# Second channel product of an MLP mixer by quarters: seven products in place of eight

## The chip, the cores and the metric

The kernel runs on one core of a Trainium2 chip. The metric is the device time of one execution in microseconds, as the median of several runs. The profile is one further execution of the same program, recorded by the hardware profiler. The engines are TensorE (PE; its weight loads are shown apart as PEld), VectorE (DVE), ScalarE (ACT), GpSimd (POOL) and SyncE (SP, which here issues transfers).

## What is computed

A linear-attention block feeds an MLP mixer. All arrays are float32; the batch is 4, with 8 heads of 48, so 384 model columns, and 768 tokens.

```
for t in range(S):                                   # per batch and head, state is 48 x 48
    cur = outer(u * k[t], v[t])
    y[t] = r[t] @ (state + cur)
    state = w[t][:, None] * state + outer(k[t], v[t])
x  = y, heads side by side                           # (4, 768, 384)
h  = relu(x^T @ w_tok1) @ w_tok2                     # w_tok1 768 x 256, w_tok2 256 x 768
u  = x + h^T
out = u + relu(u @ w_ch1) @ w_ch2                    # w_ch1 384 x 1536, w_ch2 1536 x 384
```

The change concerns the last product, relu(u @ w_ch1) @ w_ch2. Below, z is relu(u @ w_ch1).

## The kernel before

**Attention.** Tokens are cut into twelve units of 256 tokens, three to a batch. For each unit, `levels` builds a matrix of attention weights (`at`) in six doublings. A doubling is a group of small TensorE matmuls into `gram` (L246), two VectorE products that decay `k` and `r` in place (`join`, L271 and L272), and a VectorE copy under a mask out of `gram` (`pick`, L255), or a ScalarE copy for the last two. The next doubling's matmuls read the `k` and `r` that the join has written, and the join overwrites what the previous gram matmuls read. `post` then transposes k (kT, L306), forms state updates (kv_ps, L316, and twelve small VectorE operations, L333), and makes the output (y_ps, L353 and L366).

**Mixer.** `mixing(bt)` makes the pieces for one batch: `hidden` and `back` are the token products (L386, L393), `turn` transposes u into `xT`, `up` makes z, and `down` makes the output. Tokens come in three segments of 256 (SEG). For a segment, `up` runs 12 times (one 128-wide block of the 1536 hidden columns each; three matmuls of 128 x 128 weights against 256 columns, L408, and one ScalarE activation, L410, into `z`). `down` runs twice, once for each 128 tokens: 12 matmuls accumulate in one bank of PSUM, with a 128 x 128 block of z as the stationary operand and 384 columns of `wch2` moving (L417); VectorE then adds u (L421) into `o`, and SP's queue stores it (L422). z has two buffers, `o` three.

**PSUM.** Everything of the mixer, and kT of the later batches, takes turns in two banks (pool `ps_m`, tag "m"). A product can begin only when the one before the last has been read out of its bank.

**Order.** The mixer's pieces of batch bt are woven with the attention of batch bt + 1 (`woven`), in proportion to a cost written beside each piece. The framework's scheduler then fixes one order for each engine, and each engine runs its queue strictly in that order. The last batch's mixer has no attention beside it. In the first batch the four weight matrices are converted from float64 on VectorE and ScalarE (`conversion`), in scratch tiles (`d64`, `mantissa`, `exponent`), before they can be used; the first segment's down pieces are small so as to stand between conversions.

The two loops that set the order of the channel products are:

```
# first batch
pieces = downs[0][-4:] + ups[2] + downs[1] + downs[2]
# later batches
for s in range(1, S // SEG):
    pieces += ups[s] + downs[s - 1]
pieces += downs[-1]
```

Of the kernel before, what the change touches and what calls it, by code (L numbers as in the profile page):

```python
# [10 lines left out]
f32 = mybir.dt.float32  # L11
bf16 = mybir.dt.bfloat16
u8 = mybir.dt.uint8
u16 = mybir.dt.uint16
u32 = mybir.dt.uint32
# [3 lines left out]
B, H, S, D = 4, 8, 768, 48  # L19
DM = H * D  # L20
# [11 lines left out]
NJ = DCH // 128  # L32
PIECE = 512
SEG = 256


def woven(*lists):

    keyed = []
    for n, pieces in enumerate(lists):  # L40
        total, at = sum(c for c, _ in pieces), 0.0
        for i, (c, f) in enumerate(pieces):
            keyed.append(((at + c / 2) / total, n, i, c, f))
            at += c
    return [(c, f) for *_, c, f in sorted(keyed, key=lambda e: e[:3])]


def emit(pieces):
    for _, f in pieces:
        f()  # L50
# [3 lines left out]
def rwkv6_then_mixer(  # L54
# [23 lines left out]
    pe, dve, act, pool, sp = nc.tensor, nc.vector, nc.scalar, nc.gpsimd, nc.sync  # L78
# [41 lines left out]
    for l in range(4):  # L120
        b = 1 << l
        m = const.tile([128, 64 // b, 2 if l == 0 else b], f32, name=f"mask{l}")
# [5 lines left out]
        n, x = (T, 1) if l == 0 else (32, UC * A)  # L128
# [17 lines left out]
    bits64 = [wide.tile([128, 2 * PIECE], u32, name=f"d64_{i}") for i in range(2)]  # L146
    bits64 += [spare[:, ts(i, 2 * PIECE)] for i in range(2)]
    mantissas = [wide.tile([128, PIECE], u32, name=f"mantissa{i}") for i in range(2)]
    exponents = [wide.tile([128, 2, PIECE], u16, name=f"exponent{i}") for i in range(2)]
    rebias = const.tile([128, 1], f32, name="rebias")  # L150
    dve.memset(rebias, -896.0 * 128)

# [38 lines left out]
    xs = {}  # L191
# [183 lines left out]
                (0.01, lambda: load_rkw(i + 3)), (0.01, lambda: load_v(i + 3))]  # L375


    def mixing(bt):
        h1 = mpool.tile([128, DTOK // 128, DM], f32, name="h1", bufs=1)
        xT = mpool.tile([128, DM // 128, S], f32, name="xT", bufs=1)  # L380
        zs, sums = {}, {}

        def hidden(i, c):
            if c == 0:
                sums[i] = ps_m.tile([128, DM], f32, name="h1_ps", tag="m")
            pe.matmul(sums[i], wtok1[:, c, ts(i, 128)], xs[bt][:, c, :], start=(c == 0), stop=(c == C - 1))  # L386
            if c == C - 1:
                act.activation(h1[:, i, :], sums.pop(i), AF.Relu)

        def back(c):  # L390
            ps = ps_m.tile([128, DM], f32, name="h_ps", tag="m")
            for i in range(DTOK // 128):
                pe.matmul(ps, wtok2[:, i, ts(c, 128)], h1[:, i, :], start=(i == 0), stop=(i == DTOK // 128 - 1))  # L393
            x = xs[bt]
            dve.tensor_add(x[:, c, :], x[:, c, :], ps)  # L395

        def turn(c):
            ps = ps_m.tile([128, DM // 128, 128], f32, name="xT_ps", tag="m")
            for m in range(DM // 128):
                pe.transpose(ps[:, m, :], xs[bt][:, c, ts(m, 128)], ident)  # L400
            act.copy(xT[:, :, ts(c, 128)], ps)  # L401

        def up(s, jt):
            if jt == 0:
                zs[s] = mpool.tile([128, NJ, SEG], f32, name="z")
            ps = ps_m.tile([128, SEG], f32, name="z_ps", tag="m")
            for m in range(DM // 128):
                pe.matmul(ps, wch1[:, m, ts(jt, 128)], xT[:, m, ts(s, SEG)],  # L408
                          start=(m == 0), stop=(m == DM // 128 - 1))
            act.activation(zs[s][:, jt, :], ps, AF.Relu)  # L410

        def down(s, n, jts=range(NJ)):
            if jts[0] == 0:
                sums[s, n] = ps_m.tile([128, DM], f32, name="h2_ps", tag="m")
            ps = sums[s, n]
            for jt in jts:
                pe.matmul(ps, zs[s][:, jt, ts(n, 128)], wch2[:, jt, :], start=(jt == 0), stop=(jt == NJ - 1))  # L417
            if jts[-1] == NJ - 1:
                c = s * (SEG // 128) + n
                o = mpool.tile([128, DM], f32, name="o", bufs=3)  # L420
                dve.tensor_add(o, xs[bt][:, c, :], ps)  # L421
                sp.dma_start(out[bt, ts(c, 128), :], o)  # L422
# [7 lines left out]
        downs = [[(7.7, lambda s=s, n=n: down(s, n)) for n in range(SEG // 128)] for s in range(S // SEG)]  # L430
        if bt == 0:
            downs[0] = [(1.3, lambda n=n, jt=jt: down(0, n, range(jt, jt + 2)))
                        for jt in range(0, NJ, 2) for n in range(SEG // 128)]
# [12 lines left out]
    p0, p1, p2 = post(0), post(1), post(2)  # L446
# [7 lines left out]
    for bt in range(B):  # L454
        if bt == 0:
            emit(woven(turned, to_ch[:2]))
            both = [f for e in zip(ups[0], ups[1]) for f in e]
            emit(woven(both, to_ch[2:7]))
            emit(woven(downs[0][:-4], to_ch[7:]))
            pieces = downs[0][-4:] + ups[2] + downs[1] + downs[2]  # L460
        else:
            hiddens, pieces, ups, downs = mixing(bt)
            pieces = [(3.9, lambda h=h: emit(h)) for h in hiddens] + pieces + ups[0]
# [41 lines left out]
```

## Time and profile before

| | |
|---|---|
| median of 3 runs | 659.64 us (659.58 to 660.15) |
| the profiled execution's own time | 661.45 us |
| its span, first to last instruction | 659.7 us |
| mean granted TensorE clock | 0.974 |
| PE busy | 622.7 us, 94% |
| DVE busy | 273.5 us, 41% |
| ACT busy | 194.9 us, 30% |

The busy time of an engine is the union of its instructions' records. A matmul's record runs from its start to its modelled end and overlaps the next one's, so the spacing of matmuls says more than their length. In a row of the costliest groups stand the line, the engine, the operation, out<-in, the shapes and the count; then busy us and mean ns of one; then the engine's idle time just ahead of them and what ended it. In a row of the timeline stand the start, the busy time, and the merged instructions with their count. A row of the waits has who waited for whom, the sum in us, how often, and the longest.

### The profile page before, as it was taken

Reading aid. Unit: us, or ns where it says so; the run is one execution under the profiler, and the core shown is the slowest. Engines: PE = TensorE matmul, PEld = TensorE weight load, DVE = VectorE, ACT = ScalarE, POOL = GpSimd, SP = SyncE. Lnnn points to the kernel's source line nnn. Section 1 sums busy time; section 2 is a strip of 40 time slices with the busy share of each in tenths; the row PEclk is TensorE's granted clock in tenths of the full one; section 3 lists DMA queues with packets and bytes.
Section 4 is the critical chain, followed back from the end, with each engine's and each line's share of the span. In section 5 each row is a group of like instructions: output and inputs, shape, how many; then the busy total and the mean of one; then the engine's idle time right before and its main releaser. Section 6 shows DMA issues by size and latency. Waiting matters only on the chain.

```text
span 659.7 us, 18806 instructions
## 1 busy us (share of the span) xinstructions
PE 622.7 (94%) x8584; PEld 456.6 (69%) x8584; DVE 273.5 (41%) x618; ACT 194.9 (30%) x465; POOL 7.2 (1%) x32
## 2 busy tenths in 40 slices
PE   3889789999999899999999999999999999999997
PEld 3777557867866666787686666788687565886854
DVE  6889789935555326242252226243143111000000
ACT  7153554512350431423231313432121201230200
POOL 3000000000000000000000000000000000000000
PEclk9996779999999899999999999999999999999999
DMA  8236755501030320101202220000000000000000
GB/s 348 79 99 193 203 141 171 191 0 51 27 107 18 109 62 2 50 2 50 73 2 61 63 74 1 2 2 2 14 14 14 13 26 0 1 1 12 13 24 24
DMA packets 19375, 38.56 MB, mean 58 GB/s; under 512 B 2112, under 2 KB 12864, under 8 KB 19296
## 3 DMA queue, kind: packets, MB, share of 16 engines
q1 hardware_dynamic: 19152, 37.36, 18.0%
q8 instruction: 67, 1.10, 0.7%
q14 instruction: 12, 0.10, 0.0%
q10 hardware_dynamic: 144, 0.00, 0.0%
HBM read 32.64 MB, written 4.72 MB: 57 GB/s over the span
## 4 chain that ended last, share of the span: by engine, by line
PE 88%; DVE 5%; ACT 3%; DMA 2%; issue 1%; SPq 0%; DVEq 0%; ACTq 0%
PE z_ps L408 29%; PE h_ps L417 29%; PE gram L246 10%; PE h_ps L386 6%; PE h_ps L393 5%; PE y_ps L353 2%; PE y_ps L366 2%; PE gram L232 2%; PE kv_ps L316 2%; PE kT_ps L306 1%; ACT at L263 1%; DMA d<-in_w_ch_dram 1%; DVE r L272 1%; PE xT_ps L400 1%; DMA w<-in_rkw_dram 1%
## 5 line engine op out<-in xcount | busy, mean ns | idle before, releaser
L408 PE MATMUL z_ps<-xT,wch 128*128 128x256 f32 x864 | 197.2, 384 | 0.6 <-ACT xT L401 0.6
L417 PE MATMUL h_ps<-wch,z 128*128 128x384 f32 x576 | 192.9, 491 | 0.8 <-ACT kT L307 0.8
L408 PEld LDWEIGHTS z_ps<-xT,wch 128*128 128x128 f32 x864 | 160.8, 190 | 23.7 <-ACT xT L401 0.8
L417 PEld LDWEIGHTS h_ps<-wch,z 128*128 128x128 f32 x576 | 107.8, 190 | 72.0 <-ACT kT L307 1.2
L410 ACT ACTIVATE z<-z_ps 128x256 f32<-128x256 f32 x144 | 55.1, 383 | 172.2 <-PE z_ps L408 172.2
L421 DVE TENSOR_TENSOR o<-x,h_ps 128x384 f32<-128x384 f32 x24 | 13.3, 554 | 200.6 <-PE h_ps L417 200.6
L246 PEld LDWEIGHTS gram<-r,k 48*64 48x64 f32 x3840 | 74.7, 155 | 23.3 <-issue 16.1
L246 PE MATMUL gram<-r,k 48*64 48x32 f32 x3840 | 81.8, 237 | 7.7 <-issue 3.1
L271 DVE TENSOR_TENSOR k<-k,decay 112x512 f32<-112x512 f32 x36 | 24.9, 691 | 58.8 <-PE gram L246 58.8
L386 PE MATMUL h_ps<-x,wtok 128*128 128x384 f32 x96 | 40.4, 571 | 1.7 <-ACT x L372 1.6
L263 ACT COPY at<-gram 16x256 f32<-16x256 f32 (+1 forms) x72 | 31.3, 434 | 32.9 <-PE gram L246 31.5
L393 PE MATMUL h_ps<-h,wtok 128*128 128x384 f32 x96 | 36.5, 508 | 3.4 <-DVE x L395 1.7
L271 DVE TENSOR_TENSOR k<-k,w 112x512 f32<-112x512 f32 x36 | 24.7, 687 | 35.5 <-PE gram L246 30.2
L333 DVE SCALAR_TENSOR_TENSOR state<-state,w_chunk,kv_ps 128x48 f32<-128x48 f32 x160 | 29.1, 258 | 11.0 <-PE kv_ps L316 10.9
L255 DVE COPY_PREDICATED at<-mask,gram 128x512 f32<-128x512 uint8 x36 | 32.3, 897 | 0.0
L238 DVE COPY_PREDICATED at<-mask,gram 128x512 f32<-128x512 uint8 x24 | 16.3, 723 | 37.2 <-PE gram L232 37.1
L232 PE MATMUL gram<-rp,kp 48*64 48x64 f32 x768 | 21.3, 250 | 10.5 <-ACT kp L220 8.0
L232 PEld LDWEIGHTS gram<-rp,kp 48*64 48x64 f32 x768 | 17.5, 155 | 17.8 <-ACT kp L220 10.4
L386 PEld LDWEIGHTS h_ps<-x,wtok 128*128 128x128 f32 x96 | 19.9, 219 | 13.9 <-issue 3.3
L272 DVE TENSOR_TENSOR r<-r,w 112x512 f32<-112x512 f32 x36 | 24.5, 685 | 6.7 <-ACT rp L216 6.7
L393 PEld LDWEIGHTS h_ps<-h,wtok 128*128 128x128 f32 x96 | 16.6, 189 | 14.8 <-DVE x L395 2.9
L359 ACT COPY seen<-y_ps 128x2 f32<-128x2 f32 x12 | 1.9, 160 | 79.4 <-PE y_ps L353 79.4
(55 smaller groups left out, 388.0 us busy)
## 6 DMA issues: line engine op xcount, KB each, us to landing
d<-in_w_ch_dram SPq DMA_DIRECT2D x10, 512.0 KB, 4.6
vt<-in_v_dram SPq DMA_DIRECT2D x12, 384.0 KB, 3.7
out_dram<-o SPq DMA_DIRECT2D x24, 192.0 KB, 1.9
x<-in_w_ch_dram SPq DMA_DIRECT2D x8, 512.0 KB, 4.2
w<-in_rkw_dram SPq DMA_DIRECT2D x18, 192.0 KB, 3.4
k<-in_rkw_dram SPq DMA_DIRECT2D x18, 192.0 KB, 3.2
r<-in_rkw_dram SPq DMA_DIRECT2D x18, 192.0 KB, 3.4
d<-in_w_tok_dram SPq DMA_DIRECT2D x4, 512.0 KB, 9.5
```

Of the source, the lines that this page charges most:

```text
L232: pe.matmul(g[cols, q, ts(a, T)], L["kp"][rows, tokens], L["rp"][rows, tokens], start=True, stop=True)
L246: fours(lambda q, j, rows, cols: pe.matmul(g[cols, q, ts(ca, 32)], k_[rows, ds(ca * 128 + j * T, T)], right[rows, ts(2 * ca + j, 32 // b), ...
L255: dve.copy_predicated(out=dst, data=g.rearrange("p q (m b) -> p q m b", b=b), mask=masks[l].rearrange("p x t -> p (x t)").rearrange("p (m ...
L263: act.copy(at[p:p + b, :, :, n * 2 * b + b:(n + 1) * 2 * b], g[p:p + b, :, :, ts(n, b)])
L271: dve.tensor_mul(left, left, wv[:, :, 1].unsqueeze(2).to_broadcast([ROWS, n, b]))
L272: dve.tensor_mul(right, right, wv[:, :, 0].unsqueeze(2).to_broadcast([ROWS, n, b]))
L333: dve.scalar_tensor_tensor(new[:, a], state[bt, g][:, a], L["w"][:, c, a, j:j + 1], got[:, a], op0=ALU.mult, op1=ALU.add)
L386: pe.matmul(sums[i], wtok1[:, c, ts(i, 128)], xs[bt][:, c, :], start=(c == 0), stop=(c == C - 1))
L393: pe.matmul(ps, wtok2[:, i, ts(c, 128)], h1[:, i, :], start=(i == 0), stop=(i == DTOK // 128 - 1))
L408: pe.matmul(ps, wch1[:, m, ts(jt, 128)], xT[:, m, ts(s, SEG)], start=(m == 0), stop=(m == DM // 128 - 1))
L410: act.activation(zs[s][:, jt, :], ps, AF.Relu)
L417: pe.matmul(ps, zs[s][:, jt, ts(n, 128)], wch2[:, jt, :], start=(jt == 0), stop=(jt == NJ - 1))
```

## The change

The segment's product z (256 x 1536) by `wch2` (1536 x 384) is cut into quarters: z into a11, a12, a21, a22 (128 tokens by 768 hidden columns each), `wch2` into w11, w12, w21, w22 (768 by 192). The Strassen-Winograd scheme forms the four output quarters from seven products of quarters in place of eight. Each of the seven is six matmuls of a 128 x 128 block against 192 columns.

- `begin` makes three sums of z's quarters (s1, s2, s4) and one in place (a21 becomes a11 - a21): four VectorE operations of 768 elements a partition.
- `weight_sums` makes three sums of the weight's quarters once (t1, t2, t4), of 1152 elements a partition, in the scratch that the conversion has left; `weight_difference` turns w12 into w22 - w12 in place.
- p1, p4, p2, p5, p6, p7, p3 are the products, in that order, with a VectorE add or two behind each; p1 is copied out of PSUM by ScalarE first.
- The very first segment (batch 0, segment 0) keeps the undivided product. The other eleven are cut.
- z has one buffer for the first segment and one for all others; the first one's space then holds the sums. `o` is one buffer for a whole segment.
- The downs of a segment now stand right behind its ups.
- The bits, mantissas and exponents of the conversion lie in one tile, `scratch`.

```
+    def weight_sums():
+        t1, t2, t4 = w_sums
+        dve.tensor_sub(t1, w12, w11)
+        dve.tensor_sub(t2, w22, t1)
+        dve.tensor_sub(t4, w21, t2)
+
+    def weight_difference():
+        dve.tensor_sub(w12, w22, w12)
...
-                zs[s] = mpool.tile([128, NJ, SEG], f32, name="z")
+                zs[s] = halves[int((bt, s) != (0, 0))].rearrange("p (j t) -> p j t", j=NJ)
...
+        def quarters(s):
+            z = halves[1].rearrange("p (j t) -> p j t", j=NJ)
+            a11, a12, a21, a22 = (z[:, ts(j, HJ), ts(i, 128)] for i in range(2) for j in range(2))
...
+            def begin():
+                dve.tensor_add(s1, a21, a22)
+                dve.tensor_sub(s2, s1, a11)
+                dve.tensor_sub(s4, a12, s2)
+                dve.tensor_sub(a21, a11, a21)
+
+            def product(a, b):
+                ps = ps_m.tile([128, HM], f32, name="q_ps", tag="m")
+                for j in range(HJ):
+                    pe.matmul(ps, a[:, j, :], b[:, j, :], start=(j == 0), stop=(j == HJ - 1))
+                return ps
...
+            def p1():
+                o = L["o"] = mpool.tile([128, 2, DM], f32, name="o", bufs=1)
+                x = L["x"] = xs[bt][:, ts(s, 2), :]
+                act.copy(m1, product(a11, w11))
+                dve.tensor_add(o[:, 0, :HM], x[:, 0, :HM], m1)
...
+            def p4():
...
+                dve.tensor_add(o[:, 1, :HM], x[:, 1, :HM], product(a22, t4))
...
+            def p2():
...
+                dve.tensor_add(o[:, 0, :HM], o[:, 0, :HM], product(a12, w21))
...
+            def p5():
...
+                dve.tensor_add(o[:, :, HM:], x[:, :, HM:], product(s1, t1).unsqueeze(1).to_broadcast([128, 2, HM]))
...
+            def p6():
...
+                dve.tensor_add(u2, m1, product(s2, t2))
+                dve.tensor_add(o[:, 0, HM:], o[:, 0, HM:], u2)
...
+            def p7():
...
+                dve.tensor_add(u3, u2, product(a21, w12))
+                dve.tensor_add(both, both, u3.unsqueeze(1).to_broadcast([128, 2, HM]))
+                store(1)
...
+            def p3():
...
+                dve.tensor_add(o[:, 0, HM:], o[:, 0, HM:], product(s4, w22))
+                store(0)
+
+            return [(0.01, begin)] + [(1.96, p) for p in (p1, p4, p2, p5, p6, p7, p3)]
...
-            pieces = downs[0][-4:] + ups[2] + downs[1] + downs[2]
+            weight_sums()
+            pieces = downs[0][-4:] + [(0.01, weight_difference)] + downs[1] + ups[2] + downs[2]
...
-            for s in range(1, S // SEG):
-                pieces += ups[s] + downs[s - 1]
-            pieces += downs[-1]
+            for s in range(S // SEG):
+                pieces += ups[s] + downs[s]
```

**How the order moves.** The rows below are the built programs' own order; a count is of matmuls in the code. z_150 is the buffer of z that the cut segments use, z_149 the one that then holds sums, and `scratch` holds t1, t2 and t4; so `q_ps<-scratch,z_150` is p4, `q_ps<-scratch,z_149` p5 or p6, `q_ps<-wch_144,z_149` p3, and `q_ps<-wch_144,z_150` p1, p2 or p7.

TensorE at the first segment of the second batch, with the attention of the third (r_86, k_89), before:

```order
L246 MATMUL gram<-r_86,k_89 64x32 x32
L408 MATMUL z_ps<-xT,wch_143 128x256 x9
L316 MATMUL kv_ps<-vt,kT 64x48 x32
L408 MATMUL z_ps<-xT,wch_143 128x256 x9
L246 MATMUL gram<-r_86,k_89 64x32 x32
L408 MATMUL z_ps<-xT,wch_143 128x256 x9
```

And changed:

```order
L247 MATMUL gram<-r_86,k_89 64x32 x32
L427 MATMUL z_ps<-xT,wch_143 128x256 x6
L461 MATMUL q_ps<-wch_144,z_150 128x192 x6
L317 MATMUL kv_ps<-vt,kT 64x48 x32
L461 MATMUL q_ps<-scratch,z_150 128x192 x6
L247 MATMUL gram<-r_86,k_89 64x32 x32
L461 MATMUL q_ps<-wch_144,z_150 128x192 x6
L461 MATMUL q_ps<-scratch,z_149 128x192 x6
L247 MATMUL gram<-r_86,k_89 64x32 x32
```

The products stand where the next segment's ups stood, so z is multiplied as soon as it is complete, and a product of six matmuls lies on each side of the attention's groups.

VectorE at the same place, before, from the second join of that unit on:

```order
L271 TENSOR_TENSOR k_89<-k_89,decay 112x256x2
L272 TENSOR_TENSOR r_86<-r_86,decay 112x256x2
L255 COPY_PREDICATED at_95<-mask_1_116,gram 128x256x2
L273 TENSOR_TENSOR decay<-w_92 112x128
L330 COPY state<-kv_ps 128x192
L333 SCALAR_TENSOR_TENSOR state<-state,w_chunk,kv_ps 128x48 x12
L271 TENSOR_TENSOR k_89<-k_89,w_92 112x128x4
```

And changed, from `decay` on (the three rows ahead of it are the same):

```order
L274 TENSOR_TENSOR decay<-w_92 112x128
L453 TENSOR_TENSOR z_149<-z_150 128x768
L454 TENSOR_TENSOR z_149<-z_149,z_150 128x768
L456 TENSOR_TENSOR z_150<-z_150 128x6x128
L455 TENSOR_TENSOR z_149<-z_150,z_149 128x768
L471 TENSOR_TENSOR o<-x,z_149 128x192
L331 COPY state<-kv_ps 128x192
L334 SCALAR_TENSOR_TENSOR state<-state,w_chunk,kv_ps 128x48 x6
L475 TENSOR_TENSOR o<-x,q_ps 128x192
L334 SCALAR_TENSOR_TENSOR state<-state,w_chunk,kv_ps 128x48 x4
L272 TENSOR_TENSOR k_89<-k_89,w_92 112x128x4
```

The four sums of z, and the adds of p1 and p4, have come between one join and the next.

VectorE in the first batch, behind the last conversion, before:

```order
L271 TENSOR_TENSOR k_88<-k_88,decay 112x256x2
L272 TENSOR_TENSOR r_85<-r_85,decay 112x256x2
L255 COPY_PREDICATED at_94<-mask_1_116,gram 128x256x2
L273 TENSOR_TENSOR decay<-w_91 112x128
L273 TENSOR_TENSOR w_92<-decay 112x256
L272 TENSOR_TENSOR r_87<-r_87,w_93 112x512
L421 TENSOR_TENSOR o<-x,h_ps 128x384 x2
```

And changed:

```order
L272 TENSOR_TENSOR k_88<-k_88,decay 112x256x2
L390 TENSOR_TENSOR scratch<-wch_144 128x1152
L273 TENSOR_TENSOR r_85<-r_85,decay 112x256x2
L391 TENSOR_TENSOR scratch<-wch_144,scratch 128x1152
L256 COPY_PREDICATED at_94<-mask_1_116,gram 128x256x2
L392 TENSOR_TENSOR scratch<-wch_144,scratch 128x1152
...
L453 TENSOR_TENSOR z_149<-z_150 128x768
L456 TENSOR_TENSOR z_150<-z_150 128x6x128
L395 TENSOR_TENSOR wch_144<-wch_144 128x6x192
L454 TENSOR_TENSOR z_149<-z_149,z_150 128x768
L455 TENSOR_TENSOR z_149<-z_150,z_149 128x768
L441 TENSOR_TENSOR o<-x,h_ps 128x384 x2
```

The weight's sums and the first z sums stand ahead of the adds that end the first segment's undivided product.

TensorE at the end of that batch's weaving, with the third unit of the second batch (r_87, k_90), before:

```order
L353 MATMUL y_ps<-state,r_86 64x48 x32
L417 MATMUL h_ps<-wch_144,z 128x384 x6
L246 MATMUL gram<-r_87,k_90 64x32 x32
L366 MATMUL y_ps<-vt,at_95 64x48 x32
L246 MATMUL gram<-r_87,k_90 64x32 x32
L232 MATMUL gram<-rp,kp 64x64 x11
L306 MATMUL kT_ps<-ident,k_90 128x128 x8
```

And changed:

```order
L354 MATMUL y_ps<-state,r_86 64x48 x32
L247 MATMUL gram<-r_87,k_90 64x32 x32
L461 MATMUL q_ps<-wch_144,z_150 128x192 x6
L367 MATMUL y_ps<-vt,at_95 64x48 x32
L461 MATMUL q_ps<-scratch,z_149 128x192 x6
L247 MATMUL gram<-r_87,k_90 64x32 x32
L233 MATMUL gram<-rp,kp 64x64 x11
L307 MATMUL kT_ps<-ident,k_90 128x128 x8
```

Two products (p2 and p5) have come between the last two groups of gram.

More of the change, by code (lines that the diff above doesn't have):

```diff
@@ L34 @@
 SEG = 256
+HJ, HM = NJ // 2, DM // 2
 def woven(*lists):
@@ L145, in rwkv6_then_mixer @@
     spare = xpool.tile([128, C, DM], f32, name="x").rearrange("p c e -> p (c e)").bitcast(u32)
[L146 to L149, printed above, removed]
+    scratch = wide.tile([128, 8 * PIECE], u32, name="scratch")
+    bits64 = [t[:, ts(i, 2 * PIECE)] for t in (scratch, spare) for i in range(2)]
+    mantissas = [scratch[:, ts(i, PIECE)] for i in (4, 5)]
+    exponents = [scratch[:, ts(i, PIECE)].bitcast(u16).rearrange("p (two n) -> p two n", two=2) for i in (6, 7)]
     rebias = const.tile([128, 1], f32, name="rebias")
@@ L375, in post @@
                 (0.01, lambda: load_rkw(i + 3)), (0.01, lambda: load_v(i + 3))]
+    halves = [mpool.tile([128, NJ * SEG], f32, name=f"z{i}", bufs=1) for i in range(2)]
+    z_sums = [halves[0][:, ts(i, HJ * 128)].rearrange("p (j t) -> p j t", j=HJ) for i in range(3)]
+    w_sums = [scratch[:, ts(i, HJ * HM)].bitcast(f32).rearrange("p (j e) -> p j e", j=HJ) for i in range(3)]
+    parts = halves[0][:, ds(3 * HJ * 128, 3 * HM)].rearrange("p (n e) -> p n e", n=3)
+    w11, w12, w21, w22 = (wch2[:, ts(i, HJ), ts(j, HM)] for i in range(2) for j in range(2))
+    def weight_sums():
[5 more added lines that the diff above has]
+        dve.tensor_sub(w12, w22, w12)
     def mixing(bt):
@@ L410, in up, with down @@
             act.activation(zs[s][:, jt, :], ps, AF.Relu)
-        def down(s, n, jts=range(NJ)):
+        def down(n, jts):
             if jts[0] == 0:
-                sums[s, n] = ps_m.tile([128, DM], f32, name="h2_ps", tag="m")
-            ps = sums[s, n]
+                sums[n] = ps_m.tile([128, DM], f32, name="h2_ps", tag="m")
+            ps = sums[n]
             for jt in jts:
-                pe.matmul(ps, zs[s][:, jt, ts(n, 128)], wch2[:, jt, :], start=(jt == 0), stop=(jt == NJ - 1))
+                pe.matmul(ps, zs[0][:, jt, ts(n, 128)], wch2[:, jt, :], start=(jt == 0), stop=(jt == NJ - 1))
@@ L418, in down @@
             if jts[-1] == NJ - 1:
[L419 to L422, printed above, removed]
+                o = mpool.tile([128, 2, DM], f32, name="o", bufs=1) if n == 0 else sums["o"]
+                sums["o"] = o
+                dve.tensor_add(o[:, n], xs[bt][:, n, :], ps)
+                sp.dma_start(out[bt, ts(n, 128), :], o[:, n])
@@ L429, in mixing @@
         ups = [[(1.3, lambda s=s, jt=jt: up(s, jt)) for jt in range(NJ)] for s in range(S // SEG)]
[L430 to L433, printed above, removed]
+        first = [(1.3, lambda n=n, jt=jt: down(n, range(jt, jt + 2))) for jt in range(0, NJ, 2) for n in range(2)]
+        downs = [first if (bt, s) == (0, 0) else quarters(s) for s in range(S // SEG)]
         return hiddens, turned, ups, downs
@@ L459, in rwkv6_then_mixer @@
             emit(woven(downs[0][:-4], to_ch[7:]))
[L460 removed]
+            weight_sums()
+            pieces = downs[0][-4:] + [(0.01, weight_difference)] + downs[1] + ups[2] + downs[2]
         else:
             hiddens, pieces, ups, downs = mixing(bt)
[L463 to L466 removed]
+            pieces = [(3.9, lambda h=h: emit(h)) for h in hiddens] + pieces
+            for s in range(S // SEG):
+                pieces += ups[s] + downs[s]
         n = (bt + 1) * UB
```

13 lines of the change are left out of this document (added).

## The prediction

> **What bounds the kernel now.** I read the page first: busy times, the chain that ended last, the costliest groups.
>
> ```profile
> span 659.7 us, 18806 instructions
> PE 622.7 (94%) x8584; PEld 456.6 (69%) x8584; DVE 273.5 (41%) x618; ACT 194.9 (30%) x465; POOL 7.2 (1%) x32
> PE 88%; DVE 5%; ACT 3%; DMA 2%; issue 1%; SPq 0%; DVEq 0%; ACTq 0%
> L417 PE MATMUL h_ps<-wch,z 128*128 128x384 f32 x576 | 192.9, 491 | 0.8 <-ACT kT L307 0.8
> L417 PEld LDWEIGHTS h_ps<-wch,z 128*128 128x128 f32 x576 | 107.8, 190 | 72.0 <-ACT kT L307 1.2
> L421 DVE TENSOR_TENSOR o<-x,h_ps 128x384 f32<-128x384 f32 x24 | 13.3, 554 | 200.6 <-PE h_ps L417 200.6
> ```
>
> The chain is TensorE for 88%. The second channel product (L417) is 576 recorded passes; the code issues 24 outputs x 12 = 288 matmuls, so each f32 matmul runs as two passes. Busy time of pipelined passes overlaps, so I take their spacing from a stretch with nothing else in it, the last 50 us of the timeline.
>
> ```profile
> 609.50 15.70 PE L408 MATMUL z_ps<-xT,wch 128*128 128x256 f32 x72
> ...
> 625.04 31.12 PE L417 MATMUL h_ps<-wch,z 128*128 128x384 f32 x96
> ...
> 632.98 0.56 DVE L421 TENSOR_TENSOR o<-x,h_ps 128x384 f32<-128x384 f32 x1 [22.73 <-PE h_ps L417]
> 640.72 0.55 DVE L421 TENSOR_TENSOR o<-x,h_ps 128x384 f32<-128x384 f32 x1 [7.18 <-PE h_ps L417]
> ```
>
> Two outputs end 7.74 us apart; one is 24 passes, so a 384-column pass takes 322.5 ns. The 72 passes of 256 columns begin within 15.70 us less one record of 0.38 us: 15.32/71 = 215.8 ns. That is 106.7 ns for 128 columns, or 0.833 ns a column, and 2.5 ns fixed. The time of a pass goes by its columns.
>
> Then the stages, to see whether TensorE is the limit in each, and its own waits after 137 us.
>
> ```profile
> 137.00:152.00 15.00, 15.00 (x48) 8.88 (x48) 1.65 (x5) 0.38 (x1) 0.00 (x0) 1.00 0.00 0
> 152.00:242.00 90.00, 86.64 (x1803) 62.34 (x1802) 43.71 (x106) 28.14 (x68) 0.34 (x3) 0.98 0.23 68
> 242.00:402.00 160.00, 158.15 (x2264) 113.59 (x2264) 57.78 (x130) 49.23 (x122) 0.22 (x2) 1.00 0.14 39
> 402.00:562.00 160.00, 156.08 (x2053) 111.35 (x2051) 47.85 (x115) 37.28 (x89) 0.00 (x0) 1.00 0.03 9
> 562.00:657.00 95.00, 93.84 (x366) 68.60 (x363) 3.82 (x7) 14.78 (x38) 0.00 (x0) 1.00 0.03 11
> ```
>
> ```profile
> PE gram L246 <- DVE r L272: 2.3, 4, 0.6
> ...
> PE z_ps L408 <- ACT xT L401: 0.6, 2, 0.3
> ```
>
> The columns after the length are PE, PEld, DVE, ACT and POOL busy. PE is busy for 96 to 100% of every stage from 137 us on, and its seven rows of waits there (first and last shown, 2.3+2.0+1.5+1.4+0.8+0.8+0.6) hold 9.4 us. VectorE is free for two thirds of 152 to 562 us (149.3 busy of 410). So columns taken from TensorE should be time taken from the end, if VectorE's added work finds its place.
>
> **TensorE's share.** A segment of 256 tokens costs 48 passes of 384 columns now, 48 x 322.5 ns = 15.48 us. Changed, it is seven products of six matmuls, 84 passes of 192 columns. By the two numbers above one is 192 x 0.833 + 2.5 = 162.5 ns; 84 make 13.65 us. Eleven of the twelve segments change (the first stays whole): 11 x 1.83 = **20.1 us** off the path.
>
> That extrapolates 64 columns below the narrowest pass of this kind, so the weight load must fit in 162.5 ns; its record is 190 ns. The nearest rows are a start from an empty TensorE:
>
> ```profile
> L386 PEld LDWEIGHTS h_ps<-x,wtok x96: 186/190/338, 55.1 to 549.4; 128*128 128x128 f32 x96
> L386 PE MATMUL h_ps<-x,wtok x96: 486/486/1009, 55.1 to 549.7; 128*128 128x384 f32 x96
> ...
> 542.15 0.30 PEld L386 LDWEIGHTS h_ps<-x,wtok 128*128 128x128 f32 x2
> ...
> 542.16 0.91 PE L386 MATMUL h_ps<-x,wtok 128*128 128x384 f32 x2
> ```
>
> Two loads of 190 ns fit in 0.30 us: the second begins 0.11 us after the first. And the second pass begins 0.91 - 0.486 = 0.42 us after the first was issued, one pass (0.32) plus 0.10: the first pass had waited 0.10 us for its weights, not 0.19. I take a load as 0.10 to 0.11 us of occupancy and the rest as latency that overlaps. Bounds for the pass: 160 ns (columns alone) to 192 ns (a load must finish by its record before the next pass); the empty start and 215.8 ns being exactly on the line of columns put it at 162.5.
>
> A rule of the Trainium skill speaks against this: "TensorE: Matmul & The Clock Gate", Part 3, "The mechanism", has weight loads overlapping matmuls in flight only where the row group differs. By that rule each full-array pass would carry its load in front. The 215.8 ns rows, with a 128x128 load between every two passes, disagree.
>
> **VectorE's share.** Prices:
>
> ```profile
> L273 DVE TENSOR_TENSOR decay<-w 112x512 f32<-112x512 f32 x12 | 8.3, 689 | 0.3
> L273 DVE TENSOR_TENSOR w<-decay 112x256 f32<-112x256 f32 x12 | 5.0, 420 | 0.3
> L410 ACT ACTIVATE z<-z_ps 128x256 f32<-128x256 f32 x144 | 55.1, 383 | 172.2 <-PE z_ps L408 172.2
> L333 DVE SCALAR_TENSOR_TENSOR state<-state,w_chunk,kv_ps 128x48 f32<-128x48 f32 x160 | 29.1, 258 | 11.0 <-PE kv_ps L316 10.9
> out_dram<-o SPq DMA_DIRECT2D x24, 192.0 KB, 1.9
> ```
>
> 1.05 ns an element: a sum of quarters of z (768) is 0.96 us, of weights (1152) 1.36 us, a 192-wide add out of the product's bank 0.554 - 0.20 = 0.35 us. A segment adds 4 sums (3.8 us) and ten adds of which two are 384 wide (3.55+0.35 us at most), and drops two adds (1.1): +6.3 to 6.7 us. With 5.4 us for the weights VectorE rises from 273 to about 350 us. ScalarE gets one copy of 192 columns a segment, about 0.33 us by L410's row; it is far from full. The output transfers stay 24 of 192 KB; SP's queue keeps its order. There is one `o` buffer in place of three, but the next first add comes some 15 us after the store, against 1.9 us to landing. Only at the first changed segment is it close:
>
> ```profile
> 152.62 1.13 PE L246 MATMUL gram<-r,k 48*64 48x32 f32 x64
> 152.73 0.55 DVE L421 TENSOR_TENSOR o<-x,h_ps 128x384 f32<-128x384 f32 x1 [0.73 <-PE h_ps L417]
> 153.69 1.99 PE L408 MATMUL z_ps<-xT,wch 128*128 128x256 f32 x8
> ```
>
> `o` is complete at 153.3 us and would land at 155.2; product p1 takes the place of the passes at 153.69 and ends at 155.6, so no wait.
>
> The weight sums are issued behind the last conversions, into 137 to 152 us, where VectorE was busy for 1.65 of 15 us; that stretch also takes the first segment's z sums and the in-place difference (together 9.3 + 1.65 of 15). If z sums had to wait for all of the first segment's reads instead of the blocks they overwrite, some 4 us would stand on the path there: 0 to 4, and I take 0, since the order shows a second, later wait on TensorE only at the third z sum.
>
> In the other woven segments the four sums form a lump of 3.8 us in VectorE's queue, and behind it stand the add that frees p4's bank (two banks rotate, so p5 waits for it) and the attention's next join. I follow it through the first segment of the second batch, from these rows of before:
>
> ```profile
> 283.59 1.13 PE L246 MATMUL gram<-r,k 48*64 48x32 f32 x64
> 284.66 4.15 PE L408 MATMUL z_ps<-xT,wch 128*128 128x256 f32 x18
> 284.80 0.69 DVE L271 TENSOR_TENSOR k<-k,decay 112x512 f32<-112x512 f32 x1 [3.27 <-PE gram L246]
> 286.01 1.30 DVE L255 COPY_PREDICATED at<-mask,gram 128x512 f32<-128x512 uint8 x1
> 287.10 0.32 DVE L273 TENSOR_TENSOR decay<-w 112x128 f32<-112x128 f32 x1
> 288.74 1.15 PE L316 MATMUL kv_ps<-vt,kT 64*64 64x48 f32 x64
> ```
>
> TensorE: in the new order 12 up passes follow this gram, to 287.25; p1 to 289.2, kv (1.08) to 290.3, p4 to 292.2, gram to 293.3, p2 to 295.3, when p5 needs p4's bank. VectorE: free at 287.4; z is complete at about 287.9 (0.38 for the last activation by L410's row, 0.25 allowed ahead of it); four sums to 291.7, p1's add 292.1, state copy and six updates (0.18 us each by 29.1/160) to 293.5, p4's add 293.9. That is 1.4 us early. The next join ends at 295.8, its gram is wanted at 297.2. So here nothing waits. Over the eight woven segments I allow 1.5 us; the ends are 0 and 20 us (2.5 us in each, below).
>
> Something is also given back: at the end of the first batch two grams stood with only y_ps between them.
>
> ```profile
> 221.35 1.13 PE L246 MATMUL gram<-r,k 48*64 48x32 f32 x63 [0.56 <-DVE r L272]
> 223.43 0.19 PE L246 MATMUL gram<-r,k 48*64 48x32 f32 x1 [0.95 <-issue]
> ...
> 224.41 1.76 PE L306 MATMUL kT_ps<-ident,k 128*128 128x128 f32 x8 [0.27 <-DVE k L271]
> ...
> 220.00:240.00 20.00, 18.22 (x362) 12.22 (x355) 6.54 (x19) 7.00 (x17) 0.11 (x1) 0.91 0.33 100
> ```
>
> Waits of 1.8 us and a granted clock of 0.91 over 20 us (1.8 us more). Products now stand between these grams. 0 to 3.6; I take 1.5, since the 0.95 of issue is no wait for VectorE.
>
> In the last batch nothing is woven in: sums end 4.4 us after the last hidden block, p5 begins after 5.85. The very last add is 0.2 us shorter.
>
> **Sum**, against the profiled execution's 661.45 us (span 659.7): -20.1 - 0.2 + 1.5 - 1.5 = 641.1. The median of the runs, 659.64, stands 1.8 lower, so 639.3.
>
> **Rivals.** *VectorE's lump makes TensorE wait.* For it: p4's add and every join stand behind 3.8 us of sums, and the slack worked out is 1.4 us. Where twelve state updates (2.2 us) fall in as well, p5 would wait 1 to 2.5 us. 1.5 us in eight segments is 12: about 650. At 2.5 us each the whole gain is gone. Against: VectorE would still be half idle (149 + 51 of 390 us).
>
> *The weight load is the limit (slower).* If a pass cannot begin before the load's 190 ns record ends, passes come 192 ns apart: 84 x 192 = 16.1 us, +0.65 us a segment, 667 us. It decides from 15.48/84 = 184 ns on. For it: the record itself. Against: the empty start.
>
> *Loads do not overlap passes (slower).* 0.104 us in front of each: 84 x 266.5 = 22.4 against 48 x 426.5 = 20.5 us, +1.9 a segment, 681 us. The rows above exclude it nearly. It is what the rule of the Trainium skill cited above, in "TensorE: Matmul & The Clock Gate", Part 3, would make of this kernel.
>
> *The change does not do what it says*: the fixed part of a pass is larger at 192 columns, say 184 ns in all; no change, 660.
>
> **Chances.** The sum with its small terms (634 to 645): 0.75. VectorE's lump costing 6 us or more (645 to 658): 0.14. Load limit 0.05, no overlap 0.01, no change 0.03, below 634 (more given back) 0.02. The range 634 to 650 takes 0.75 and two thirds of the second case. A difference under 0.2% is about what cannot be told from none here. Faster: 0.75 + 0.02 + 0.13 = 0.90; same 0.03; slower 0.07.
>
> **What would show it.** 924 passes of q_ps, 162.5 ns apart in the tail, a quarter segment 13.65 us long there; VectorE near 350 us; few waits of q_ps on `o`. A spacing of 184 ns or more, or rows of several us "q_ps <- DVE o" or "gram <- DVE", would prove me wrong.

## The result, and the profile after

The changed kernel takes 637.45 us (median of 4 runs, 637.35 to 639.3), the kernel before 659.89 us beside it (4 runs, 659.58 to 663.98): a ratio of 0.9653, 95% interval 0.9611 to 0.9694, or 22.4 us less. The profiled execution took 637.35 us.

The page after, the lines that answer to those shown of before:

```profile
span 635.6 us, 19813 instructions
PE 605.2 (95%) x8980; PEld 508.2 (80%) x8980; DVE 341.8 (54%) x743; ACT 198.3 (31%) x476; POOL 7.2 (1%) x32
PE 90%; ACT 3%; DVE 3%; DMA 2%; issue 1%; SPq 0%; ACTq 0%; DVEq 0%
L461 PE MATMUL q_ps<-wch,z 128*128 128x192 f32 x528 | 94.9, 330 | 0.0
L461 PE MATMUL q_ps<-scratch,z 128*128 128x192 f32 x396 | 71.2, 330 | 0.2 <-ACT kT L308 0.2
L453 DVE TENSOR_TENSOR z<-z 128x768 f32<-128x768 f32 x11 | 10.5, 959 | 66.6 <-ACT z L429 66.6
```

TensorE is still the chain, now for 90%. The second channel product is 528 + 396 = 924 passes of 192 columns beside the first segment's 48 whole ones. VectorE has risen from 273.5 to 341.8 us and is no bound.

A segment of the last batch, from TensorE's timeline:

```profile
589.25 2.11 PE L461 MATMUL q_ps<-wch,z 128*128 128x192 f32 x12
591.20 2.11 PE L461 MATMUL q_ps<-scratch,z 128*128 128x192 f32 x12
593.15 2.11 PE L461 MATMUL q_ps<-wch,z 128*128 128x192 f32 x12
595.10 4.06 PE L461 MATMUL q_ps<-scratch,z 128*128 128x192 f32 x24
599.00 4.06 PE L461 MATMUL q_ps<-wch,z 128*128 128x192 f32 x24
602.90 1.46 PE L427 MATMUL z_ps<-xT,wch 128*128 128x256 f32 x6
```

The starts are what counts: 589.25 to 602.90 is 13.65 us for 84 passes, 162.5 ns each, and a product of 12 passes is 1.95 us. The two whole outputs of a segment took 15.48 us before.

TensorE's waits from 137 us to the end (who waited for whom, sum in us, times, longest):

```profile
PE h_ps L412 <- DVE x L414: 1.3, 4, 0.4
PE gram L247 <- DVE r L273: 1.2, 2, 0.6
PE z_ps L427 <- ACT xT L420: 0.5, 2, 0.3
PE kT_ps L307 <- DVE k L272: 0.4, 1, 0.4
PE xT_ps L419 <- DVE x L414: 0.3, 1, 0.3
PE q_ps L461 <- ACT kT L308: 0.2, 1, 0.2
```

They hold 3.9 us, against 9.4 before. No product waits for a bank that an add frees ("q_ps <- DVE o" isn't there), and 1.5 us of "gram <- issue" have gone.

**How kernels are compared below.** Whole times of one program differ by some us between executions. In after's two profiles the whole times are 0.9 us apart, and from the first z_ps matmul on only 0.03; e7 and e9 are 3.5 us apart, and not at all from there on. That matmul begins anywhere from 104 to 109 us, behind the conversion. So beside the medians the table gives, from each profiled execution, the time from the start of the first z_ps matmul to the end of the last matmul (end less start, "from z on"). Before's is 656.16 - 105.59; it was profiled once, and its runs scatter by about 8 us in each of the later sets.

| kernel | median us (runs) | ratio to before on the same chip, 95% | from z on, us |
|---|---|---|---|
| before | 659.89 (4) | | 550.57 |
| after | 637.45 (4) | 0.9653, 0.9611 to 0.9694 | 526.83 |
| after, again | 638.24 (6) | 0.9613, 0.9580 to 0.9645 | 526.86 |
| e1, undivided, changed order | 664.22 (12) | 1.001, 0.9982 to 1.0037 | 553.19 |
| e2, the same in small pieces | 656.90 (6) | 0.9916, 0.9885 to 0.9947 | 546.01 |
| e8, before in small pieces | 656.04 (6) | 0.9874, 0.9837 to 0.9911 | 544.91 |
| e3, eight quarter products | 657.71 (10) | 0.992, 0.9896 to 0.9943 | 546.41 |
| e4, seven products, no sums | 639.50 (6) | 0.9645, 0.9614 to 0.9676 | 527.03 |
| e5, sums doubled | 640.35 (4) | 0.9639, 0.9599 to 0.9679 | 529.97 |
| e10, doubled, p4's add behind all | 658.41 (6) | 0.9926, 0.9890 to 0.9963 | 547.36 |
| e6, passes of 96 columns | 692.85 (2) | 1.0426, 1.0360 to 1.0492 | 581.83 |
| e7, all twelve segments cut | 638.14 (6) | 0.9602, 0.9565 to 0.9638 | 526.20 |
| e9, the same, p2 ahead of p4 | 637.47 (6) | 0.9604, 0.9575 to 0.9634 | 526.20 |

E1 to e4 shared one set of runs of before (663.23 us, 21 runs), e5 to e8 another (664.55, 11), the second run of after, e9 and e10 a third (663.56, 13).

### The profile page after: what moved, and what is told of

It is laid out like the page before. It is cut to its first block, busy times and chain, and to the rows that moved or that the text cites. A ratio compares the mean times of both kernels' runs of the same rounds, so it can differ in the third digit from the quotient of the medians.

```text
span 635.6 us, 19813 instructions
## 1 busy us (share of the span) xinstructions
PE 605.2 (95%) x8980; PEld 508.2 (80%) x8980; DVE 341.8 (54%) x743; ACT 198.3 (31%) x476; POOL 7.2 (1%) x32
## 4 chain that ended last, share of the span: by engine, by line
PE 90%; ACT 3%; DVE 3%; DMA 2%; issue 1%; SPq 0%; ACTq 0%; DVEq 0%
PE z_ps L427 31%; PE q_ps L461 24%; PE gram L247 10%; PE h_ps L405 6%; PE h_ps L412 5%; PE h_ps L437 2%; PE kv_ps L317 2%; PE gram L233 2%; PE y_ps L367 2%; PE y_ps L354 2%; PE kT_ps L307 1%; ACT at L264 1%; DMA scratch<-in_w_ch_dram 1%; PE xT_ps L419 1%; DMA w<-in_rkw_dram 1%
## 5 line engine op out<-in xcount | busy, mean ns | idle before, releaser
L461 PE MATMUL q_ps<-wch,z 128*128 128x192 f32 x528 | 94.9, 330 | 0.0
L461 PEld LDWEIGHTS q_ps<-wch,z 128*128 128x128 f32 x528 | 86.1, 190 | 1.4
L461 PE MATMUL q_ps<-scratch,z 128*128 128x192 f32 x396 | 71.2, 330 | 0.2 <-ACT kT L308 0.2
L461 PEld LDWEIGHTS q_ps<-scratch,z 128*128 128x128 f32 x396 | 64.2, 190 | 1.3 <-ACT kT L308 0.6
L453 DVE TENSOR_TENSOR z<-z 128x768 f32<-128x768 f32 x11 | 10.5, 959 | 66.6 <-ACT z L429 66.6
L405 PE MATMUL h_ps<-x,wtok 128*128 128x384 f32 x96 | 39.1, 557 | 1.7 <-ACT x L373 1.6
L334 DVE SCALAR_TENSOR_TENSOR state<-state,w_chunk,kv_ps 128x48 f32<-128x48 f32 x160 | 30.5, 256 | 4.4 <-PE kv_ps L317 4.3
```

Source lines behind the costliest of these rows:

```text
L334: dve.scalar_tensor_tensor(new[:, a], state[bt, g][:, a], L["w"][:, c, a, j:j + 1], got[:, a], op0=ALU.mult, op1=ALU.add)
L461: pe.matmul(ps, a[:, j, :], b[:, j, :], start=(j == 0), stop=(j == HJ - 1))
```

## Experiments

The theory: 20.1 us are columns that TensorE no longer passes; the sums are free as long as the adds that free the banks don't stand behind them; the rest comes from what stands between the attention's groups. The rivals: the order of the pieces, the size of the pieces, or the sums costing something that another gain covers.

**Where do the 3 to 4 us beyond the columns come from: e1, e2, e8.** The diff also moves a segment's downs ahead of the next segment's ups, and replaces two pieces of 7.7 us by seven of 1.96. e1 takes the new order with the undivided product in two pieces, e2 the same in eight pieces of three matmuls; neither makes sums.

```
-        def quarters(s):
+        def undivided(s):
...
+            def whole(n, jts):
...
+                for j in jts:
+                    pe.matmul(L[n], z[:, j, ts(n, 128)], wch2[:, j, :], start=(j == 0), stop=(j == NJ - 1))
```

with jts = range(12) at a cost of 7.74 (e1) or range(j, j + 3) at 1.94 (e2).

> The changed kernel's order (downs of a segment right behind its ups, one buffer of z), but the undivided product: 24 matmuls of 384 columns in two pieces of 7.7, no sums. If the gain is the columns (theory), a segment costs 15.48 us again and the time is that of before less what the order alone gives back: 657 to 660. If a good part of the 22 us came from the order and the smaller pieces (rival), it is 640 to 652.

> As e1, but the undivided product is woven in eight pieces of three matmuls (1.9 us each, as long as one of the seven products). The trace of the change shows 2.0 us more gained in the first batch and 1.3 in the second than eleven times 1.83. If products between the attention's groups give that (theory), e2 is 1 to 3 us under e1, 655.5 to 658.5. If it came from something else, a clock dip of one execution or the order of the segments, e2 equals e1.

e8 is the kernel before, its own order kept, with the pieces cut alone:

```
-        downs = [[(7.7, lambda s=s, n=n: down(s, n)) for n in range(SEG // 128)] for s in range(S // SEG)]
+        downs = [[(1.93, lambda s=s, n=n, j=j: down(s, n, range(j, j + 3))) for n in range(SEG // 128)
+                  for j in range(0, NJ, 3)] for s in range(S // SEG)]
```

> The kernel before, in its own order, with each undivided output woven in four pieces of three matmuls in place of one of twelve. e2 had these pieces in the changed order and was 4.6 us shorter by trace than before, e1 in large pieces was not. If the size of the pieces alone does it (theory), this kernel is 4 to 6 us under before. If it takes the new order of the segments as well (rival), within 1.5 us of before.

From z on, e1 is 2.6 us above before, e2 4.6 below, e8 5.7 below; by the medians e2 is 6.3 and e8 8.5 us below, and e1 isn't told from before. E1 thus missed its 657 to 660, and e2 gained 7.3 us on e1 by the medians where 1 to 3 had been expected; e8 came as forecast by trace. So the order isn't the source; the size of the pieces is, and it is worth that without any quarter product. Where it comes from shows in 180 to 232 us, the end of the first batch. The rows of the windows are, in this order, of before, e1, e2, e8 and after; the columns behind the length are PE, PEld, DVE, ACT and POOL busy, the granted clock, the DMA share and GB/s.

```profile
180.00:232.00 52.00, 48.68 (x1057) 33.63 (x1058) 26.19 (x67) 16.75 (x40) 0.22 (x2) 0.97 0.26 74
```
```profile
180.00:232.00 52.00, 50.22 (x1076) 37.81 (x1076) 28.08 (x75) 20.43 (x51) 0.34 (x3) 0.93 0.24 67
```
```profile
180.00:232.00 52.00, 51.95 (x1065) 38.64 (x1064) 26.22 (x67) 20.62 (x51) 0.17 (x2) 1.00 0.26 71
```
```profile
180.00:232.00 52.00, 52.00 (x1044) 34.38 (x1042) 27.32 (x68) 16.75 (x40) 0.22 (x2) 1.00 0.27 74
```
```profile
180.00:232.00 52.00, 51.34 (x1190) 44.16 (x1189) 30.39 (x75) 21.01 (x54) 0.22 (x2) 1.00 0.25 71
```

Before loses 3.3 us of TensorE there and a clock of 0.97 over 52 us (1.6 us more); e1 gives up 1.8 us and 0.07 x 52 = 3.6. The three kernels with pieces of 2 us lose 0 to 0.7 and have the full clock. In before's timeline TensorE waits at three places in that stretch, of which the prediction counted the last alone (221 to 228 us). These are the other two:

```profile
193.99 1.09 PE L306 MATMUL kT_ps<-ident,k 128*128 128x128 f32 x8 [0.45 <-DVE k L271]
...
206.43 0.56 PE L246 MATMUL gram<-r,k 48*64 48x32 f32 x25 [0.56 <-DVE r L272]
207.53 0.78 PE L246 MATMUL gram<-r,k 48*64 48x32 f32 x39 [0.54 <-issue]
```

With a whole output of 7.7 us as the smallest piece, two attention groups that wait on VectorE's joins stand side by side. With pieces of 2 us a piece stands between any two groups of gram that follow a join there, as in e2:

```profile
208.01 1.14 PE L247 MATMUL gram<-r,k 48*64 48x32 f32 x64
209.08 2.20 PE L452 MATMUL q_ps<-wch,z 128*128 128x384 f32 x6
211.21 1.13 PE L247 MATMUL gram<-r,k 48*64 48x32 f32 x64
```

From 137 us on TensorE's waits are 3.9 us in e2 as in e8, against 9.4 in before.

**Does the division alone gain: e3.** Eight products of quarters, six matmuls of 192 columns each, in the new order, no sums.

```
+            def eighth(n, e, h):
...
+                    pe.matmul(L["ps"], z[:, j, ts(n, 128)], wch2[:, j, ts(e, HM)], start=(j == 0), stop=(j == NJ - 1))
```

> Eight products of quarters, 192 columns wide, two accumulated into each output quarter; no sums. The same columns as undivided in twice as many passes with twice the weight loads. By 162.5 ns a pass a segment is 96 x 0.1625 = 15.60 us, 0.12 more than undivided: eleven make +1.3 us on e2, so 657 to 660. If the load's record of 190 ns limited a pass (rival), 18.4 us a segment, +32 us.

A segment of the last batch in e3:

```profile
574.33 15.76 PE L452 MATMUL q_ps<-wch,z 128*128 128x192 f32 x96
589.93 15.70 PE L427 MATMUL z_ps<-xT,wch 128*128 128x256 f32 x72
```

96 passes in 15.60 us are 162.5 ns each, as in after. From z on e3 is 0.4 us above e2 and 19.6 above after. So halving the columns brings nothing; the missing eighth product does. By columns its twelve passes are 11 x 1.95 = 21.5 us, 1.9 more than came: 1.0 of it is waits (2.9 us in e3 from 137 us on, 3.9 in after), the rest stands in no wait of the view and stays open.

**What do the sums cost: e4.** Seven products of plain quarters; neither the sums of z nor those of the weight are made, so the output isn't the reference's.

```
-            s1, s2, s4 = z_sums
-            t1, t2, t4 = w_sums
+            s1, s2, s4 = a21, a11, a12
+            t1, t2, t4 = w12, w22, w21
...
-            return [(0.01, begin)] + [(1.96, p) for p in (p1, p4, p2, p5, p6, p7, p3)]
+            return [(1.96, p) for p in (p1, p4, p2, p5, p6, p7, p3)]
```

> The seven products without any sum of z or of the weight: they read plain quarters, so the output is another; the adds behind the products stay. If VectorE's sums are hidden (theory), within 0.7 us of the change, 636.7 to 638. If the lump of sums costs about 1.5 us in the woven segments (rival), 625 to 630.

```profile
PE 603.1 (95%) x8980; PEld 505.1 (79%) x8980; DVE 299.1 (47%) x695; ACT 198.3 (31%) x476; POOL 7.2 (1%) x32
```

VectorE does 42.7 us less than in after and TensorE has the same 8980 passes; from z on e4 takes 527.03 us, after 526.83. The sums cost nothing that can be seen. The median, 639.50, lies above the 636.7 to 638 expected, but before stood 3.3 us higher in that set too (663.23 against 659.89), and the ratio's interval holds after's 0.9653.

**How near is the lump to the point where it costs: e5, then e10.** e5 makes s4 four more times in each cut segment.

```
                 dve.tensor_sub(s4, a12, s2)
+                for _ in range(4):
+                    dve.tensor_sub(s4, a12, s2)
```

> The change with s4 made four times more in each segment (same values): VectorE's lump of sums doubles, +3.8 us a segment. In the trace of the change p4's add ends 0.95 us before p5 begins in the three segments of the last batch, and 1.8 to 3.2 us before it in seven of the woven ones (the first changed segment makes its sums 10 us early). If the lump is a wait once it outgrows that slack (theory), p5 is late by 2.8 us in each of the last three and by 0.6 to 2.0 in seven others: 14 to 19 us in all, about 652 to 657. If VectorE's idle half takes it up (rival), under 2 us: 637 to 640.

It came out 3.1 us above after from z on, a fifth of the cost expected (the median is 640.35, not 652 to 657). VectorE's timeline in the last batch tells why:

```profile
595.42 0.95 DVE L455 TENSOR_TENSOR z<-z,z 128x768 f32<-128x768 f32 x1
596.28 0.35 DVE L473 TENSOR_TENSOR o<-x,z 128x192 f32<-128x192 f32 x1
596.55 0.95 DVE L457 TENSOR_TENSOR z<-z,z 128x768 f32<-128x768 f32 x1
597.42 0.35 DVE L477 TENSOR_TENSOR o<-x,q_ps 128x192 f32<-128x192 f32 x1
597.68 0.95 DVE L457 TENSOR_TENSOR z<-z,z 128x768 f32<-128x768 f32 x1
```

L457 is the repeated sum. The scheduler did not leave the eight sums in one lump: p1's add (L473) stands ahead of the four repeats and p4's (L477) behind the first of them, so p4's bank is freed behind five sums, not eight. My theory had taken the order of the code for the order of the queue, and fell. e10 forces the order: the same repeats, and behind them a copy into the place of `o` that p4's add writes (`o` is taken there and no longer in p1).

```
+                L["o"] = mpool.tile([128, 2, DM], f32, name="o", bufs=1)
+                dve.tensor_copy(L["o"][:, 1, :HM], halves[0][:, ds(2 * HJ * 128, HM)])
```

> As e5, VectorE's sums doubled, but the last of the added operations writes 192 columns into the place in o that p4's add then overwrites, so that p4's add must stand behind all of them. e5 came out only 3.1 us longer by trace than the change, and its order shows the added operations behind the adds of p1 and p4. If it was that order which kept them harmless (theory), p5 now begins about 3.2 us late in each of the last three segments and 1 to 2.6 us late in seven woven ones: 15 to 25 us over the changed kernel. If VectorE has room wherever the work stands (rival), within 4 us of it, as e5.

The median rose by 20.2 us over after's on the same chip (658.41 against 638.24), from z on by 20.5. In the waits from 130 us on:

```profile
PE gram L247 <- DVE r L273: 6.9, 7, 1.5
PE q_ps L465 <- DVE o L483: 2.8, 4, 0.8
PE q_ps L465 <- DVE o L479: 2.5, 5, 1.0
```

and in the last batch:

```profile
611.53 2.11 PE L465 MATMUL q_ps<-wch,z 128*128 128x192 f32 x12
...
614.45 2.22 PE L465 MATMUL q_ps<-scratch,z 128*128 128x192 f32 x12 [0.80 <-DVE o L483]
...
616.28 0.26 DVE L460 COPY o<-z 128x192 f32<-128x192 f32 x1
616.58 0.35 DVE L479 TENSOR_TENSOR o<-x,q_ps 128x192 f32<-128x192 f32 x1
...
616.99 1.24 PE L465 MATMUL q_ps<-scratch,z 128*128 128x192 f32 x6 [0.32 <-DVE o L479]
```

So VectorE's work costs by its place, not by its amount: nearly the same amount was 3.1 us where the adds stood inside it and 20.5 us behind it. The total was as expected and its split was not. In the last batch p2's add now stands ahead of p4's, p5 takes that bank, and p5 and p6 begin 0.97 and 0.59 us late (614.45 against 611.53 + 1.95; 616.99 against 614.45 + 1.95) where I had worked out 3.2 us in all; the woven segments lost more, by the joins that stand behind the lump (6.9 us of gram's waits) and by the clock (last section).

**Is the weight load near its limit: e6.** Each product in two halves of 96 columns, the same weights loaded again for the second.

```
-                for j in range(HJ):
-                    pe.matmul(ps, a[:, j, :], b[:, j, :], start=(j == 0), stop=(j == HJ - 1))
+                for e in range(2):
+                    for j in range(HJ):
+                        pe.matmul(ps[:, ts(e, HM // 2)], a[:, j, :], b[:, j, ts(e, HM // 2)],
+                                  start=(j == 0), stop=(j == HJ - 1))
```

> The change with each matmul of 192 columns issued as two of 96, each with its weights loaded again: 168 passes a segment. By columns alone a pass is 82.5 ns and a segment 13.9 us (+2 us in all). If a load occupies 0.105 to 0.11 us (theory), passes come 107 to 110 ns apart, a segment is 18.0 to 18.5 us in the last batch, and the whole +48 to +53 us: 685 to 692. If loads cannot overlap passes (rival), 190 ns and more a pass, 32 us a segment, over 830.

```profile
632.74 2.81 PE L462 MATMUL q_ps<-wch,z 128*128 128x96 f32 x24
...
646.11 5.52 PE L462 MATMUL q_ps<-wch,z 128*128 128x96 f32 x48
651.47 1.70 PE L427 MATMUL z_ps<-xT,wch 128*128 128x256 f32 x7
```

168 passes take 651.47 - 632.74 = 18.73 us, 111.5 ns each. By columns they would take 96 x 0.833 + 2.5 = 82.5 ns. Something other than the columns is the limit here. That it is the load, at 0.11 us and not at the 0.19 of its record, fits the 0.11 us between two loads that the prediction read from an empty start; no run tells it apart from another fixed cost of a pass. At 192 columns a pass has 51 ns to spare over it. Spacing, segment and median (692.85) all came slightly above the ranges expected.

**The twelfth segment: e7 and e9.** e7 cuts the first segment too; its z sums go to a spare tile of the conversion, and the weight sums and the difference are made ahead of its products. Its weaving differs as well: the segment's products stand beside the first attention unit of the second batch, not between conversions. e9 is e7 with p2, which needs no weight sum, ahead of p4 in that segment.

```
-        downs = [first if (bt, s) == (0, 0) else quarters(s) for s in range(S // SEG)]
+        downs = [quarters(s) for s in range(S // SEG)]
...
-            emit(woven(downs[0][:-4], to_ch[7:]))
+            emit(to_ch[7:])
             weight_sums()
-            pieces = downs[0][-4:] + [(0.01, weight_difference)] + downs[1] + ups[2] + downs[2]
+            weight_difference()
+            emit(woven(levels(UB), downs[0]))
+            pieces = downs[1] + ups[2] + downs[2]
```

> The first segment too goes by seven products; its z sums lie in the spare tile of the conversion, m1, u2 and u3 in the rest of the scratch, and the weight's sums and difference stand ahead of it. One more segment by columns: -1.83 us (theory), 635 to 637. If VectorE, which has weight sums and z sums to make just behind the conversions, holds TensorE up there (rival), no gain or a loss: 638 to 642.

> All twelve segments by seven products, and in the first one p2, which needs no sum, stands ahead of p4, which in e7 waited 0.8 us for the third weight sum. By e7's stages (0.96 us less than the change up to the second batch) and this wait: 1.4 to 1.8 us under the changed kernel from the first hidden block on. If VectorE only passes the wait on to p4 or p5 (rival), 0.5 to 1.0 us under it.

In e7, VectorE and TensorE at the first p4:

```profile
143.17 1.37 DVE L393 TENSOR_TENSOR scratch<-wch,scratch 128x1152 f32<-128x1152 f32 x1
144.68 2.19 PE L462 MATMUL q_ps<-scratch,z 128*128 128x192 f32 x12 [0.83 <-DVE scratch L393]
```

p4 waits 0.83 us for t4, so of the 1.83 us of columns 1.0 is left, and from z on 0.63 us in the end. The median, 638.14, lies in the rival's range and not in the theory's, and by the intervals e7 isn't told from after. In e9 that wait is gone and another has come, in the waits:

```profile
PE q_ps L462 <- DVE o L480: 0.7, 1, 0.7
```

L480 is p2's add, which stands behind the weight sums on VectorE and frees the bank that p5, the fourth product, needs. From z on e9 equals e7 (526.20), so the rival was right: the wait was passed on. Against after on the same chip e9 is 0.8 us lower (637.47 against 638.24), 0.12% with overlapping runs, which isn't told from no change; the traces' 0.63 to 0.66 us speak for a real but tiny gain. Nothing tried beats the changed kernel by more.

## Why the prediction was right, by its own steps

Predicted were 639.3 us (634 to 650); 637.45 came. By the traces the difference from z on is 23.7 us: 20.1 for the columns, 4.6 from the pieces (e2 against before), less about 1 that stays open (after is 19.2 below e2 instead of 20.1).

- **Columns, -20.1.** Right to what the trace resolves: 162.5 ns and 13.65 us, where 64 columns had been extrapolated. The load's occupancy of 0.10 to 0.11 us, read from an empty start, agrees with the 0.11 of e6; with passes 162.5 ns apart, the rival that the 190 ns record sets the spacing is out. So is the one without overlap. The Trainium skill, "TensorE: Matmul & The Clock Gate", Part 3, "The mechanism", says that loads overlap only with matmuls of another row group. That does not agree with this trace: these full-array passes, a load for each, come at the time of their columns, 162.5 ns. The same page, Part 2, "LDWEIGHTS (loading the stationary operand)", gives columns / 1.2 in ns, from which 107 ns for 128 is an estimate; e6's 111.5 agrees with that nearly.
- **VectorE, about 350 us.** 341.8. A sum of 768 is 0.96 us as priced.
- **Weight sums and first z sums in 137 to 152 us at nothing.** Right: e4 without them isn't faster. The cover is thin, though: needed 16 us earlier (p4 begins 35.5 us behind the first z_ps matmul in e7, 51.3 in after), they made TensorE wait 0.83 us.
- **The lump of sums.** The worked segment gave p4's add 1.4 us to spare. In the trace of after, the same place:

```profile
284.26 0.35 DVE L475 TENSOR_TENSOR o<-x,q_ps 128x192 f32<-128x192 f32 x1
...
286.72 2.11 PE L461 MATMUL q_ps<-scratch,z 128*128 128x192 f32 x12
```

The add ends at 284.61, p5 begins at 286.72: 2.1 us. In the last batch it is the least:

```profile
592.67 0.95 DVE L455 TENSOR_TENSOR z<-z,z 128x768 f32<-128x768 f32 x1
593.80 0.35 DVE L475 TENSOR_TENSOR o<-x,q_ps 128x192 f32<-128x192 f32 x1
```

594.15 against p5's 595.10, 0.95 us; there the prediction had compared only the end of the sums with p5's start, and left out the add. The rival's mechanism is real (e10), but its condition is about one microsecond more of work ahead of p4's add than this kernel has.

- **New waits, +1.5.** None came in sum: from 137 us on after's waits are 3.9 us, as e2's are; the row that e2 lacks (kT on `k`, 0.4) stands in e4 too, which has no sums. What after lacks against e2 is about 1 us, and it stands in no wait of the view; so the term's size is near and its reason isn't shown.
- **Given back, -1.5.** This is the mis-sized term: 4.6 against the one profile of before, 5.7 for the pieces alone (e8). I took the waits at 221 to 228 us alone and halved them; the batch had two more such places (0.45, and 0.56 + 0.54 us), the half clock cost its whole 1.6 us, and the 0.95 of "issue" which I left out as no wait for VectorE went as well. The stage's own row, quoted there, would have bounded it: 152 to 242 us held 90 - 86.64 = 3.4 us without TensorE and a clock of 0.98, 1.8 us more.
- **The offset to the median, -1.8.** Before's profiled execution stood 1.8 us above its median; after's stands on it (637.35, 637.45). So 3.1 us too little given back and 0.5 too much for new waits were in part hidden by an offset that did not carry over; that the median came within 1.9 us is in this part luck. 641.1 was forecast for the profiled execution; it is 637.35.

## What to carry to other kernels

Where TensorE is busy for 96% of every stage and a pass goes by its columns (here down to 192), count columns: one product in eight was worth what the count said, and operand sums on another engine were free because they fitted between two deadlines, not because that engine was half idle. Before adding such work, find the queued operation that frees the next PSUM bank and measure how early it ends (here 0.95 us at the least), in the built order and not in the code's. And when a change also alters the size of the pieces that are woven between waiting groups, price that apart, by every wait of the stage: here it was worth 5.7 us by trace with no other change (e8).

## What was unexpected of the hardware

TensorE's clock fell by half in mid-kernel after short waits, not after a long idle time. In before, the waits of 0.56, 0.95 and 0.27 us from 220 us on, which the prediction quotes, are followed by this window:

```profile
225.00:229.00 4.00, 4.00 (x62) 2.47 (x62) 0.68 (x1) 1.56 (x3) 0.00 (x0) 0.62 0.50 135
```

TensorE is busy all through it, at a clock of 0.62; in each of the three microseconds from 225 to 228 us it is 0.50. e10 shows the same, in TensorE's timeline and the windows:

```profile
334.08 0.85 PE L247 MATMUL gram<-r,k 48*64 48x32 f32 x42 [1.54 <-DVE r L273]
335.56 4.71 PE L465 MATMUL q_ps<-scratch,z 128*128 128x192 f32 x17 [0.62 <-DVE o L479]
```
```profile
334.00:341.00 7.00, 6.30 (x65) 6.22 (x66) 4.87 (x20) 0.00 (x0) 0.00 (x0) 0.76 0.01 2
```

Waits of 1.54 and 0.62 us, with a group of small matmuls between them, and then a clock of 0.76 over 7 us: 17 passes of 192 columns took 4.71 us, where 17 x 162.5 ns are 2.76. So two microseconds of waits cost 0.24 x 7 = 1.7 more. Not every such wait does it. In e10 a wait of gram of 1.28 us, up to 443.47 us, is followed by a clock of 0.72 over 443 to 449 us, while one of 1.29 us up to 291.09 and one of kT of 1.38 up to 223.62 left the clock at 1.00, and so did the 0.80 and 0.32 us between full passes in the last batch. What decides isn't shown. The Trainium skill, "TensorE: Matmul & The Clock Gate", Part 1, "HAM oscillation — how this bites in real kernels", speaks of idle gaps over 3.4 us, which these rows do not need; its next section, "A second HAM failure mode: psum-queue depth-cycling", has frequent short idle times between groups bring it, and that agrees in so far as single short waits are enough here; neither tells these cases from those in which the clock stayed.
